# Reordering the opening, the first layers and the early bursts of a retention and two-layer kernel

## The chip, the cores and the metric

The kernel runs on one core of one Trainium2 chip. The metric is the device time of one execution in microseconds (us); less is better.

## The reference

```python
scores = (1/8) * q @ k.transpose(0, 1, 3, 2)          # 8 batches, 8 heads, 576 positions, 64 wide
gamma  = 1 - 2.0 ** (-5 - arange(8))                   # one decay per head
Dmat   = where(rel >= 0, gamma ** rel, 0)              # rel = i - j
x      = ((scores * Dmat) @ v) -> (4608 tokens, 512)
h      = x @ w_in                                      # 512 -> 2048
out    = maximum(0.01 * h, h) @ w_out                  # 2048 -> 512, float32
```

## The kernel before, in words

**Units and groups.** The 4608 tokens are cut into 36 units of 128 tokens (two chunks of 64) and into 9 groups of 4 units. A batch has nine chunks of 64, so a unit can straddle two batches; then each of its loads is two transfers. Retention is done chunk by chunk with a running state, all products are in float16 with float32 sums.

**Per unit u.** `load(u)` brings q, k and v in float32 (three transfers of 256 KB; `ld_pool` has six buffers). `cast_k` (L172, ScalarE) casts k, `cast_q` (L175) and `cast_v` (L179) multiply q and v by decay tables; q and k go to the tile `qk16`, v to `v16`. q and k are then transposed, in the opening by TensorE (`transpose_pe`, L200, with the copy `transposed`, L207), later by a DMA that SP issues (`transpose_dma`, L183). `scores(u)` (L215, L224) makes the 64-wide score blocks and the k-v products of both chunks in one PSUM tile. VectorE masks the scores (`masks`, L233) and advances the running state (`state`, L255, L257, L260, L261), and `state_cast` (L273, L276) makes it float16. The outputs need the mask, the state of the chunk before and the transposed q. Two forms exist: `outputs_acc` (L321, L333) sums both parts in PSUM and `x_copy` (L341, ScalarE) writes the tile `xT`; `outputs` (L291, L302) keeps the parts apart, ScalarE copies one (`own`, L355) and VectorE adds the other to it (`add`, L360), which gives `xT`.

**The two layers per group.** The first layer (L373) multiplies `w_in` with `xT` and ScalarE applies the leaky function (L387), giving `gt`. It comes in pieces: `h_block` (512 tokens), `h_half(g, a, fb)` (256 tokens: half a of group g; piece fb of the hidden width), `h_unit(u, fb)` (the 128 tokens of one unit, four column blocks, of group u // 4). The second layer of group 0 is the plain product `wide` (L423, 16 steps). Groups 1 to 8 use a seven-product scheme (`seven`, L483), with sums of weights (`mix_weights`, L448) and of activations (`mix`, L467) made by VectorE. After its first product ScalarE copies the sum out of PSUM (`keep("k1", "p1")`, L495), and the second product adds to the same PSUM tile, so it waits for that copy. Other results leave through L497, L506 and L508.

**What sets the order.** The schedule is written by hand: each engine runs its instructions in the order in which the code issues them, and waits where a value or a buffer is not ready. Buffers: `acc` (four PSUM tiles for transposes, fillers, first and second layer), `ot` and `sc` one PSUM tile each. `keep_warm(n)` issues n filler products on TensorE (L549, 128x512, no use of the result).

**Stages.** (1) The opening: units 0 to 3, with loads issued by SP and GpSimd, `w_in` in four quarters behind them on GpSimd's queue, and `w_out` last. (2) The first layers of groups 0 and 1, between which the units 4 to 7 are worked in: `turn(u, x)` transposes k (1) or q (0), `settle(u)` is state and mask, `finish(u)` is `outputs_acc` and `x_copy`. (3) `wide` and then `seven(1)`, with `ahead(u)` (casts by ScalarE and GpSimd, transpose by SP) and `burst(u)` (scores of u, outputs of u - 1, state, mask, own, add) placed between the products. Transfers of later units are issued by SP, in the order of the code: transposes, loads and stores share that queue. (4) Groups 2 to 8 in a loop, each with its four bursts. Units 8 to 11 are the tokens of group 2, so its first layer waits for the add of unit 11, which `burst(12)` holds.

The bursts of stage 3 stand as follows: unit 8 (scores only) after step 9 of `wide`; 9 after `wide`; 10, 11 and 12 after the products 1, 3 and 6 of `seven(1)` (counted from 0), the last being the final product. `ahead(u + 3)` and `load(u + 5)` follow each of the bursts 9 to 11.

Of the kernel before, what the change touches and what calls it, by code (L numbers as in the profile page):

```python
# [18 lines left out]
def kernel(  # L19
# [9 lines left out]
    nc = tc.nc  # L29
# [54 lines left out]
    def behind(dma, *others):  # L84
        for o in others:
            tc.add_manual_dep(
                dma.ins,
                o.ins.name,
                mybir.DependencyInfo(
                    mybir.DependencyClass.Sync, mybir.DependencyReason.DATA  # L90
                ),
                reason="order of loads",
            )
# [17 lines left out]
    last_load = {}  # L111
# [7 lines left out]
    def load(u, eng=None, after=None):  # L119
        for x in (1, 0, 2):  # L120
            t = ld_pool.tile([P, H, D], FP, name=f"t32_{x}")
            t32[u, x] = t
            c = 2 * u
            same = c % CB + 1 < CB
            e = eng[x] if isinstance(eng, dict) else eng or nc.sync
            engs = e if isinstance(e, tuple) else (e,)
            n = H // len(engs)
            for j, rows in ((0, P),) if same else ((0, CH), (1, CH)):
                b, w = (c + j) // CB, (c + j) % CB
                for i, e in enumerate(engs):  # L130
                    hs = slice(n * i, n * i + n)
                    d = e.dma_start(  # L132
                        out=t[CH * j : CH * j + rows, hs],
                        in_=(q, k, v)[x][b, hs, CH * w : CH * w + rows, :].rearrange(
                            "h t d -> t h d"
                        ),
                    )
                    if after is not None:
                        behind(d, *after)
                        after = None  # L140
                    last_load[u, x] = d

# [31 lines left out]
    def cast_q(u, eng):  # L174
        eng.tensor_tensor(out=qk16[u][:, 0], in0=t32[u, 0], in1=decay(u, 0), op=MUL)  # L175

    def cast_v(u, eng):
        v16[u] = a_pool.tile([P, H, D], F16, name="v16")
        eng.tensor_tensor(out=v16[u], in0=t32[u, 2], in1=decay(u, 1), op=MUL)  # L179
# [26 lines left out]
    def transposed(u, x, copy):  # L206
        copy(out=qkT[u][:, x], in_=tr[u, x])  # L207

    def scores(u):
        a = sc_pool.tile([P, 2, 2, NP, CH], FP, name="sc")  # L210
        sc_tiles[u] = a
        for p in range(NP):
            for g in range(2):
                for j in range(2):
                    nc.tensor.matmul(  # L215
                        out=a[half(j), g, 0, p, :],
                        lhsT=qkT[u][half(g), 1, p, half(j)],
                        rhs=qkT[u][half(g), 0, p, half(j)],
                        start=True, stop=True, skip_group_check=True,
                    )  # L220
        for p in range(NP):
            for j in range(2):
                for g in range(2):
                    nc.tensor.matmul(  # L224
                        out=a[half(g), j, 1, p, :],
                        lhsT=qk16[u][half(j), 1, 2 * p + g, :],
                        rhs=v16[u][half(j), 2 * p + g, :],
                        start=True, stop=True, skip_group_check=True,
                    )
# [316 lines left out]
    def keep_warm(n):  # L546
        t = acc_pool.tile([P, 1, TOK], FP, name="acc")
        for _ in range(n):
            nc.tensor.matmul(out=t[:, 0, :], lhsT=idle[:, 0:P], rhs=idle, start=True, stop=True)  # L549
# [7 lines left out]

    keep_warm(7)
    load(0, {1: nc.sync, 0: (nc.sync, nc.gpsimd), 2: nc.gpsimd})
    for u in range(1, 4):  # L560
        load(u, nc.gpsimd)
    for f in range(3):
        load_w_in(f)
    load(4, nc.gpsimd)
# [6 lines left out]
    cast_k(0)  # L571
    transpose_pe(0, 1)
    transposed(0, 1, act_copy)
    keep_warm(2)
    cast_q(0, nc.vector)
    cast_v(0, nc.vector)
    transpose_pe(0, 0)
    transposed(0, 0, act_copy)
    keep_warm(2)
    cast_k(1)  # L580
    cast_q(1, nc.vector)
    cast_v(1, nc.vector)
    for u in range(4):
        n = u + 1
        scores(u)
        state(u, 0)
        state_cast(u, dve_copy, (0,))
        masks(u)
        state(u, 1)
        if n < 4:  # L590
            transpose_pe(n, 1)
            transpose_pe(n, 0)
            transposed(n, 1, act_copy)
            transposed(n, 0, act_copy)
            keep_warm(1)
        if n < 3:
            cast_k(n + 1)
            cast_q(n + 1, nc.vector)
            cast_v(n + 1, nc.vector)
        state_cast(u, act_copy, (1,))  # L600
        if n < 4:
            outputs_acc(u)
            x_copy(u)
            keep_warm(2)
# [3 lines left out]
        for a, fb in items:  # L608
            h_half(g, a, fb)

    def casts(u, eng):
        cast_k(u)
        cast_q(u, nc.vector)
        cast_v(u, eng)

    def turn(u, x):
        transpose_pe(u, x)
# [2 lines left out]
    def settle(u):  # L620
        state(u, 0)
        state_cast(u, dve_copy, (0,))
        masks(u)
        state(u, 1)
        state_cast(u, act_copy, (1,))

    def finish(u):
        outputs_acc(u)
        x_copy(u)

    halves(0, (0, 0), (0, 1))
    finish(3)
    halves(0, (0, 2), (0, 3), (1, 0), (1, 1))
    casts(4, nc.vector)
    halves(0, (1, 2), (1, 3))
    turn(4, 1)
    halves(0, (0, 4), (0, 5))
    turn(4, 0)
    halves(0, (1, 4))
    casts(5, nc.vector)  # L640
    halves(0, (1, 5))
    scores(4)
    settle(4)
    halves(0, (0, 6), (0, 7))
    finish(4)
    turn(5, 1)
    halves(0, (1, 6))
    turn(5, 0)
    casts(6, nc.vector)
    halves(0, (1, 7))  # L650
    scores(5)
    settle(5)
    h_unit(4, 0)
    turn(6, 1)
    h_unit(4, 1)
    finish(5)
    turn(6, 0)
    casts(7, nc.vector)
    h_unit(5, 0)
    scores(6)  # L660
    settle(6)
    turn(7, 1)
    h_unit(5, 1)
    finish(6)
    halves(1, (0, 4))
    turn(7, 0)
    halves(1, (0, 5))
    scores(7)
    settle(7)
    halves(1, (0, 6))  # L670
    finish(7)
    load(8, after=(w_out_loads[2],))
    load(9)
    halves(1, (0, 7))
    for n in range(4):
        mix_weights(n, 0)
        mix_weights(n, 1)
        halves(1, (1, 2 * n), (1, 2 * n + 1))
# [34 lines left out]
    def step(u):  # L713
# [2 lines left out]
        ahead(u + 2)  # L716


    at = {
        0: lambda: (ahead(8), load(10)),  # L720
        3: lambda: (ahead(9), load(11)),
        6: lambda: (ahead(10), load(12)),
        9: lambda: (burst(8, False), ahead(11), load(13)),
        12: lambda: mixes(1, 0),
        14: lambda: mixes(1, 1),
    }
    for n in range(16):
        wide(n // 4, n % 4)
        if n in at:
            at[n]()  # L730

    def early(u):
        burst(u)
        if u < 12:
            ahead(u + 3)
            load(u + 5)

    early(9)
    mixes(1, 2)
    seven(  # L740
        1,
        {
            1: [lambda: early(10)],
            3: [lambda: early(11)],
            6: [lambda: early(12)],
        },
    )

    first = [f for i in range(4) for f in (i, i + HF)]
    second = [f for i in range(4, 8) for f in (i, i + HF)]  # L750
# [46 lines left out]
```

## Time and profile before

| | |
|---|---|
| median of 13 executions | 304.89 us (303.5 to 307.95) |
| the profiled execution | 304.37 us, of which the span of the trace is 302.6 |
| TensorE, matmuls | 286.0 us busy, 95% of the span |
| TensorE, weight loads | 193.5 us, 64% |
| VectorE | 169.9 us, 56% |
| ScalarE | 144.5 us, 48% |
| GpSimd | 106.0 us, 35% |
| mean granted TensorE clock | 0.977 of full |
| data moved | 50.01 MB, 165 GB/s |

The span runs from the first to the last instruction; the rest of the execution's time lies around it. PE is TensorE, PEld its weight load, DVE VectorE, ACT ScalarE, POOL GpSimd, SP the sync engine; a "q" behind an engine is its queue that issues transfers. L12 is line 12 of the kernel. In a timeline row the columns are start and length in us, engine, line, operation, result and operands, count, and in brackets the idle time of that engine before it with what ended it. Times in the text are from the start of the span.

### The profile page before, as it was taken

What the parts mean: (1) busy time and instruction counts of PE and PEld (TensorE: products, weight loads), DVE (VectorE), ACT (ScalarE), POOL (GpSimd) and SP (SyncE); (2) the same over time, 40 slices, a digit from 0 to 9 for tenths busy, and PEclk for the clock granted to TensorE, in tenths of its full rate; (3) what the DMA queues carried; (4) which work ended last, traced back from release to release, by engine and by line L of the source; (5) the groups of instructions that cost most, each with busy time, mean ns of one, the idle gap of its engine ahead of it and who ended that gap; (6) DMA issues with size and microseconds to landing.
All of it is one profiled execution on the core that took longest, in us unless ns stands there. A gap on an engine that the chain in (4) does not pass through costs nothing.

```text
span 302.6 us, 9351 instructions
## 1 busy us (share of the span) xinstructions
PE 286.0 (95%) x4068; PEld 193.5 (64%) x4068; DVE 169.9 (56%) x291; ACT 144.5 (48%) x254; POOL 106.0 (35%) x126
## 2 busy tenths in 40 slices
PE   7699987999996999999999999999999999999994
PEld 3358876854683458745864686478547854884583
DVE  2843475905994259545856564677458636740342
ACT  4646664643412773276237714762475167306510
POOL 8947901405643323433334333333334414000000
PEclk9859999999997999999999999999999999999999
DMA  7898999339999986896689767957896451012003
GB/s 205 240 197 176 312 207 221 69 79 237 247 239 209 310 182 142 183 254 140 135 193 250 163 149 213 217 131 167 220 220 109 97 175 37 4 42 99 0 2 139
DMA packets 130298, 50.01 MB, mean 165 GB/s; under 512 B 119728, under 2 KB 124464, under 8 KB 130256
## 3 DMA queue, kind: packets, MB, share of 16 engines
q1 hardware_dynamic: 123824, 39.20, 55.7%
q0 software_dynamic: 6144, 10.09, 15.1%
q8 instruction: 32, 0.52, 0.7%
q10 hardware_dynamic: 288, 0.11, 0.1%
q14 instruction: 10, 0.08, 0.1%
HBM read 36.81 MB, written 9.44 MB: 153 GB/s over the span
## 4 chain that ended last, share of the span: by engine, by line
PE 87%; DVE 3%; POOL 3%; DMA 2%; ACT 1%; issue 1%; DVEq 0%; ACTq 0%; POOLq 0%
PE acc L373 41%; PE acc L483 33%; PE acc L423 5%; POOL t L132 3%; PE sc L215 3%; DMA t<-in_v_dram 2%; PE sc L224 1%; PE ot L291 1%; PE ot L302 1%; DVE s L233 1%; PE ot L321 1%; DVE s L257 1%; ACT gt L387 0%; PE acc L200 0%; ACT k L495 0%
## 5 line engine op out<-in xcount | busy, mean ns | idle before, releaser
L373 PE MATMUL acc<-xT,w_in 128*128 128x512 f16 (+2 forms) x736 | 132.8, 337 | 3.7 <-DVE xT L360 2.8
L387 ACT ACTIVATE gt<-acc 128x512 f16<-128x512 f32 x144 | 85.6, 597 | 55.4 <-PE acc L373 54.0
L373 PEld LDWEIGHTS <-w_in 128*128 128x128 f16 x736 | 68.5, 99 | 57.1 <-issue 5.9
L483 PEld LDWEIGHTS <-gt 128*128 128x128 f16 x640 | 61.9, 98 | 10.8 <-issue 1.7
L233 DVE TENSOR_TENSOR s<-sc,cs 128x512 f16<-128x512 f32 x36 | 24.7, 685 | 47.5 <-PE sc L224 47.5
L483 PE MATMUL acc<-w_out,gt 128*128 128x256 f16 x384 | 45.9, 273 | 1.6 <-ACT k L495 1.4
L273 POOL CAST st<-s 128x512 f16<-128x512 f32 x21 | 12.8, 609 | 86.3 <-DVE s L257 55.9
L175 POOL TENSOR_TENSOR qk<-t,cs 128x512 f16<-128x512 f32 x28 | 30.1, 1074 | 30.4 <-DMA t<-in_q_dram 14.9
L355 ACT COPY own<-ot 128x512 f32<-128x512 f32 x28 | 16.4, 585 | 38.1 <-PE ot L302 30.5
L179 POOL TENSOR_TENSOR v<-t,cs 128x512 f16<-128x512 f32 x28 | 31.9, 1140 | 0.7 <-PE acc L373 0.4
L483 PE MATMUL acc<-w_mix,gt 128*128 128x256 f16 x256 | 30.6, 273 | 0.0
L467 DVE TENSOR_TENSOR mix<-gt 128x1024 f16<-128x1024 f16 x16 | 14.2, 891 | 28.8 <-ACT gt L387 28.8
L483 PE MATMUL acc<-w_mix,mix 128*128 128x256 f16 x256 | 29.3, 273 | 0.0
L172 ACT CAST qk<-t 128x512 f16<-128x512 f32 x36 | 22.3, 621 | 10.7 <-DMA t<-in_k_dram 10.7
L483 PEld LDWEIGHTS <-mix 128*128 128x128 f16 x256 | 25.0, 98 | 2.9
L360 DVE TENSOR_TENSOR xT<-ot,own 128x512 f16<-128x512 f32 x28 | 19.1, 682 | 0.3 <-ACT own L355 0.3
L257 DVE TENSOR_TENSOR s<-sc,s 128x256 f32<-128x256 f32 x40 | 16.7, 419 | 4.5 <-PE sc L224 4.0
L508 DVE TENSOR_TENSOR osb<-acc,u 128x512 f32<-128x512 f32 (+1 forms) x17 | 11.1, 656 | 9.0 <-PE acc L483 9.0
L215 PEld LDWEIGHTS <-qkT 64*64 64x64 f16 x576 | 7.8, 109 | 12.3 <-issue 10.1
L467 DVE TENSOR_TENSOR mix<-mix,gt 128x1024 f16<-128x1024 f16 x16 | 14.8, 932 | 0.5
L276 POOL CAST st<-s 128x256 f16<-128x256 f32 x7 | 3.2, 454 | 32.8 <-DVE s L261 18.2
L423 PE MATMUL acc<-w_out,gt 128*128 128x512 f16 x64 | 14.2, 379 | 0.0
(52 smaller groups left out, 245.6 us busy)
## 6 DMA issues: line engine op xcount, KB each, us to landing
out_dram<-osb SPq DMA_DIRECT2D x17, 512.0 KB, 3.8
t<-in_k_dram SPq DMA_DIRECT2D x26, 256.0 KB, 3.5
t<-in_q_dram SPq DMA_DIRECT2D x25, 256.0 KB, 4.0
t<-in_v_dram SPq DMA_DIRECT2D x25, 256.0 KB, 4.8
w_in<-in_moe_w_in_dram POOLq DMA_DIRECT2D x8, 256.0 KB, 9.1
w_out<-in_moe_w_out_dram POOLq DMA_DIRECT2D x4, 512.0 KB, 9.6
t<-in_v_dram POOLq DMA_DIRECT2D x7, 256.0 KB, 4.9
t<-in_k_dram POOLq DMA_DIRECT2D x6, 256.0 KB, 4.9
```

Of the source, the lines that this page charges most:

```text
L172: nc.scalar.copy(out=qk16[u][:, 1], in_=t32[u, 1])
L175: eng.tensor_tensor(out=qk16[u][:, 0], in0=t32[u, 0], in1=decay(u, 0), op=MUL)
L179: eng.tensor_tensor(out=v16[u], in0=t32[u, 2], in1=decay(u, 1), op=MUL)
L215: nc.tensor.matmul(out=a[half(j), g, 0, p, :], lhsT=qkT[u][half(g), 1, p, half(j)], rhs=qkT[u][half(g), 0, p, half(j)], start=True, stop=T ...
L233: nc.vector.tensor_tensor(out=s16s[u], in0=sc_tiles[u][:, :, 0], in1=mask_sb.unsqueeze(1).unsqueeze(1).to_broadcast([P, 2, NP, CH]), op=MUL,)
L257: nc.vector.tensor_tensor(out=to, in0=st, in1=carry[0], op=ADD)
L360: nc.vector.tensor_tensor(out=x_of(u).rearrange("q (c g) t -> q c g t", g=2), in0=ot_tiles[u][:, :, NP : 2 * NP].rearrange("q g (c j) t -> ...
L373: nc.tensor.matmul(out=hps[:, n, :], lhsT=w_in16[:, c, f * P : (f + 1) * P], rhs=xT[g][:, c, ts], start=(c == 0), stop=(c == NP - 1),)
L387: nc.scalar.activation(out=out, in_=in_, func=mybir.ActivationFunctionType.Lrelu)
L423: nc.tensor.matmul(out=ys[tb], lhsT=g_t[0][:, f, tb * P : (tb + 1) * P], rhs=w_out16[:, f, :], start=(f == 0), stop=(f == NF - 1),)
L467: nc.vector.tensor_tensor(out=z[:, fs], in0=a[:, fs], in1=b[:, fs], op=op)
L483: nc.tensor.matmul(out=r[name][:, tb, :], lhsT=lhs[:, f, tb * P : (tb + 1) * P], rhs=rhs[:, f, :], start=fresh and n == 0, stop=f == HF - ...
```

## The change

Loads of k for units 1 and 3 go from GpSimd's queue to SP's; that of unit 3 is issued when the one of unit 1 has landed. In the opening, VectorE casts q and v of unit 1 after state and mask of unit 0 and no longer before; TensorE does the outputs of unit 0 between the two transposes of unit 1; and there are 12 more fillers. Outputs of unit 3 stay where they were. For units 4 to 7, k is cast earlier, q and v casts follow the state and mask of the unit before, the float16 cast of the second chunk's state follows `x_copy`, and the places of some first-layer pieces change; two pieces `h_half(1, 1, 0)` and `(1, 1, 1)` become `h_unit(6, 0)` and `h_unit(7, 0)`. In stage 3, units 8 and 9 are prepared before `wide`, unit 8's burst stands after step 4 of `wide`, 9's after step 9, 10's after `wide`, and 11's and 12's after products 0 and 4 of `seven(1)`. Each `ahead` and `load` comes with its burst, so the cast of k of unit 13 now stands ahead of `seven(1)`. All other computation is the same.

```diff
@@ -135,8 +135,8 @@
                             "h t d -> t h d"
                         ),
                     )
-                    if after is not None:
-                        behind(d, *after)
+                    if after is not None and (x in after or not isinstance(after, dict)):
+                        behind(d, *(after[x] if isinstance(after, dict) else after))
                         after = None
                     last_load[u, x] = d
 
@@ -557,8 +557,9 @@
 
     keep_warm(7)
     load(0, {1: nc.sync, 0: (nc.sync, nc.gpsimd), 2: nc.gpsimd})
-    for u in range(1, 4):
-        load(u, nc.gpsimd)
+    load(1, {1: nc.sync, 0: nc.gpsimd, 2: nc.gpsimd})
+    load(2, nc.gpsimd)
+    load(3, {1: nc.sync, 0: nc.gpsimd, 2: nc.gpsimd}, {1: (last_load[1, 1],)})
     for f in range(3):
         load_w_in(f)
     load(4, nc.gpsimd)
@@ -571,34 +572,42 @@
     cast_k(0)
     transpose_pe(0, 1)
     transposed(0, 1, act_copy)
-    keep_warm(2)
+    keep_warm(3)
     cast_q(0, nc.vector)
     cast_v(0, nc.vector)
     transpose_pe(0, 0)
     transposed(0, 0, act_copy)
-    keep_warm(2)
+    keep_warm(3)
     cast_k(1)
-    cast_q(1, nc.vector)
-    cast_v(1, nc.vector)
     for u in range(4):
         n = u + 1
         scores(u)
+        if not u:
+            keep_warm(3)
         state(u, 0)
         state_cast(u, dve_copy, (0,))
         masks(u)
+        if not u:
+            cast_q(1, nc.vector)
+            cast_v(1, nc.vector)
         state(u, 1)
         if n < 4:
             transpose_pe(n, 1)
+            transposed(n, 1, act_copy)
+            if not u:
+                keep_warm(3)
+                outputs_acc(0)
+                x_copy(0)
+                keep_warm(1)
             transpose_pe(n, 0)
-            transposed(n, 1, act_copy)
             transposed(n, 0, act_copy)
-            keep_warm(1)
+            keep_warm(2 if not u else 3)
         if n < 3:
             cast_k(n + 1)
             cast_q(n + 1, nc.vector)
             cast_v(n + 1, nc.vector)
         state_cast(u, act_copy, (1,))
-        if n < 4:
+        if 0 < u < 3:
             outputs_acc(u)
             x_copy(u)
             keep_warm(2)
@@ -608,10 +617,9 @@
         for a, fb in items:
             h_half(g, a, fb)
 
-    def casts(u, eng):
-        cast_k(u)
+    def cast_qv(u):
         cast_q(u, nc.vector)
-        cast_v(u, eng)
+        cast_v(u, nc.vector)
 
     def turn(u, x):
         transpose_pe(u, x)
@@ -622,57 +630,64 @@
         state_cast(u, dve_copy, (0,))
         masks(u)
         state(u, 1)
-        state_cast(u, act_copy, (1,))
 
     def finish(u):
         outputs_acc(u)
         x_copy(u)
+        state_cast(u, act_copy, (1,))
 
     halves(0, (0, 0), (0, 1))
-    finish(3)
-    halves(0, (0, 2), (0, 3), (1, 0), (1, 1))
-    casts(4, nc.vector)
-    halves(0, (1, 2), (1, 3))
+    outputs_acc(3)
+    x_copy(3)
+    halves(0, (0, 2), (0, 3), (1, 0))
+    cast_k(4)
+    cast_qv(4)
+    halves(0, (1, 1), (1, 2), (1, 3))
     turn(4, 1)
     halves(0, (0, 4), (0, 5))
     turn(4, 0)
-    halves(0, (1, 4))
-    casts(5, nc.vector)
-    halves(0, (1, 5))
+    halves(0, (1, 4), (1, 5))
+    cast_k(5)
     scores(4)
     settle(4)
+    cast_qv(5)
     halves(0, (0, 6), (0, 7))
     finish(4)
     turn(5, 1)
+    cast_k(6)
     halves(0, (1, 6))
     turn(5, 0)
-    casts(6, nc.vector)
     halves(0, (1, 7))
     scores(5)
     settle(5)
+    cast_qv(6)
     h_unit(4, 0)
     turn(6, 1)
+    cast_k(7)
     h_unit(4, 1)
     finish(5)
     turn(6, 0)
-    casts(7, nc.vector)
     h_unit(5, 0)
     scores(6)
     settle(6)
+    cast_qv(7)
+    h_unit(5, 1)
     turn(7, 1)
-    h_unit(5, 1)
+    halves(1, (0, 4))
     finish(6)
-    halves(1, (0, 4))
     turn(7, 0)
     halves(1, (0, 5))
     scores(7)
     settle(7)
-    halves(1, (0, 6))
+    halves(1, (0, 6), (0, 7))
     finish(7)
     load(8, after=(w_out_loads[2],))
     load(9)
-    halves(1, (0, 7))
-    for n in range(4):
+    h_unit(6, 0)
+    mix_weights(0, 0)
+    mix_weights(0, 1)
+    h_unit(7, 0)
+    for n in range(1, 4):
         mix_weights(n, 0)
         mix_weights(n, 1)
         halves(1, (1, 2 * n), (1, 2 * n + 1))
@@ -716,35 +731,30 @@
         ahead(u + 2)
 
 
+    def early(u, out=True):
+        burst(u, out)
+        if 8 < u < 12:
+            ahead(u + 3)
+            load(u + 5)
+
+    ahead(8)
+    load(10)
+    ahead(9)
+    load(11)
     at = {
-        0: lambda: (ahead(8), load(10)),
-        3: lambda: (ahead(9), load(11)),
-        6: lambda: (ahead(10), load(12)),
-        9: lambda: (burst(8, False), ahead(11), load(13)),
-        12: lambda: mixes(1, 0),
-        14: lambda: mixes(1, 1),
+        2: lambda: (ahead(10), load(12)),
+        4: lambda: (burst(8, False), ahead(11), load(13)),
+        9: lambda: early(9),
+        11: lambda: mixes(1, 0),
+        13: lambda: mixes(1, 1),
     }
     for n in range(16):
         wide(n // 4, n % 4)
         if n in at:
             at[n]()
-
-    def early(u):
-        burst(u)
-        if u < 12:
-            ahead(u + 3)
-            load(u + 5)
-
-    early(9)
+    early(10)
     mixes(1, 2)
-    seven(
-        1,
-        {
-            1: [lambda: early(10)],
-            3: [lambda: early(11)],
-            6: [lambda: early(12)],
-        },
-    )
+    seven(1, {0: [lambda: early(11)], 4: [lambda: early(12)]})
 
     first = [f for i in range(4) for f in (i, i + HF)]
     second = [f for i in range(4, 8) for f in (i, i + HF)]
```

## The prediction

> **What bounds it.** I read the chain of waits first, then the wait before each TensorE group in the timeline, then the clock by microsecond. TensorE carries 87% of the chain, and from 25 us on it is nearly gapless, so only its gaps, its slow clock and the opening can give time. Columns of the chain: start, length, what.
>
> ```profile
> 1.27 8.80 POOL t L132 x10
> ...
> 10.07 6.96 DMA t<-in_v_dram
> ...
> 17.67 0.42 DVE s L257
> ```
>
> GpSimd issues ten loads, then unit 3's v lands at 17.03 and VectorE's state of unit 2 follows: the opening hangs on that load. The windows show (after the span and PE, PEld, DVE, ACT, POOL) the clock, DMA share and GB/s.
>
> ```profile
> 10.00:11.00 1.00, 0.00 (x0) 0.00 (x0) 0.97 (x3) 0.62 (x1) 1.00 (x2) 1.00 1.00 320
> ...
> 13.00:14.00 1.00, 1.00 (x9) 0.54 (x9) 0.92 (x3) 0.65 (x2) 1.00 (x2) 0.61 0.77 154
> ...
> 23.00:24.00 1.00, 1.00 (x8) 0.82 (x7) 0.97 (x3) 0.00 (x0) 0.67 (x1) 0.77 1.13 302
> ```
>
> ```profile
> 94.00:95.00 1.00, 0.00 (x0) 0.00 (x0) 0.97 (x3) 0.00 (x0) 0.62 (x1) 1.00 0.88 202
> ...
> 95.00:96.00 1.00, 0.45 (x2) 0.17 (x2) 0.50 (x1) 0.00 (x0) 0.61 (x1) 0.57 1.19 270
> ...
> 98.00:99.00 1.00, 1.00 (x5) 0.41 (x4) 0.00 (x0) 0.10 (x2) 0.00 (x0) 0.72 1.21 260
> ```
>
> TensorE idles at 10 us, the clock falls to half at 13.2 (0.61 of full in that slice) and is back at 23.46 (0.77); it falls again at 95.1 and is back at 98.56. The timeline gives the gaps (start, length; in brackets the idle time before and its releaser):
>
> ```profile
> 44.46 1.05 PE L373 MATMUL acc<-xT,w_in 128*128 128x128 f16 x16 [0.67 <-ACT xT L341]
> ...
> 48.30 0.31 PE L321 MATMUL ot<-s,v 64*64 64x64 f16 x8 [1.19 <-DVE s L233]
> ...
> 53.24 0.31 PE L321 MATMUL ot<-s,v 64*64 64x64 f16 x8 [0.55 <-DVE s L233]
> ```
>
> ```profile
> 78.03 0.62 ACT L172 CAST qk<-t 128x512 f16<-128x512 f32 x1
> ...
> 79.32 0.58 ACT L495 COPY k<-acc 128x512 f32<-128x512 f32 x1 [0.67 <-PE acc L483]
> ...
> 79.69 1.39 SPq L132 DMA_DIRECT2D t<-in_k_dram  x2
> ...
> 79.95 1.91 PE L483 MATMUL acc<-w_out,gt 128*128 128x256 f16 x16 [0.67 <-ACT k L495]
> ...
> 84.14 0.62 ACT L172 CAST qk<-t 128x512 f16<-128x512 f32 x1 [0.94 <-DMA t<-in_k_dram]
> ...
> 95.55 5.95 PE L373 MATMUL acc<-xT,w_in 128*128 128x512 f16 x20 [2.82 <-DVE xT L360]
> ```
>
> In the first layers 1.19 and 0.55 us go to late masks (units 6 and 7) and 0.67 to a late xT (unit 5). In the second stage product 1 waits 0.67 for ScalarE's copy of product 0, and the layer of group 2 starts 2.82 us late, behind the add of burst(12).
>
> **The skill.** "TensorE: Matmul & The Clock Gate", Part 1, says that a free-running window of about 3.4 us of low activity halves the clock. The trace agrees: 98.56 - 95.1 is one window, 23.46 - 13.2 = 10.2 is three. Its "Architectural detail" says that ScalarE and VectorE take instructions strictly in order; the lines above fit (the copy at 79.32 after the cast at 78.03), though that copy was waiting for TensorE, so this trace doesn't prove it. "DMA: Bandwidth & Descriptors", "Queues, rings and completion order", says that each engine takes one packet from each queue in turn. With both queues loaded, from 3.25 to 3.50 us:
>
> ```profile
> q10 hardware_dynamic: 91, 0.05, 65.6%
> ...
> q1 hardware_dynamic: 120, 0.03, 52.6%
> ```
>
> 91 packets against 120: near one for one, so it agrees.
>
> **Opening, part by part.** Moving k of units 1 and 3 to SP takes two issues (0.9 us each) off GpSimd, so v of unit 3 is issued at 8.3 instead of 10.07; with before's latencies (4.9 for q just ahead, 7.0 for it) it lands between 13.2 and 15.3. SP gains two issues, before the wait for load(8), which ends at 46.79: covered. k of unit 1 now shares the DMA engines with GpSimd's stream: behind 1,536 packets of unit 0 it starts at about 4.0; alone 1,024 packets need 1.0 us (272 per 0.25 us), in turn with GpSimd's 89 packets per us 11.5 us. GpSimd's stream shows a share of 0.956 where SP's shows 1.22, so there are free slots: I take 3.5 to 4 us, landing near 8, against 7.4 before. Its casts end near 8.7, TensorE wants it at 8.4.
>
> VectorE does unit 0's state and mask before unit 1's casts (timeline durations: state 0.42, its cast 0.29, mask 0.68, q and v casts 0.69): from scores at 7.7, mask(0) ends near 9.05 instead of 11.2. Then q1, v1, the state add, q2 and v2 end near 12.3; unit 1's state and mask to 14.55; q3 and v3 to 16.0 instead of 17.66. Outputs(2) can then start at 17.4, not 19.07. The 12 more fillers cost 0.21 each at full clock, 2.6 us, all in gaps where TensorE waits for masks or casts; behind them wait transposes and outputs, and without cover I would charge up to 0.6. They put five fillers in each stretch in which before had three or fewer, so the clock should hold. In the half-clock stretch from 19.07 to 23.46 that is worth about 2.0.
>
> What is late next is w_in. GpSimd's issues wait for its landings:
>
> ```profile
> 19.56 0.68 POOL L132 DMA_DIRECT2D t<-in_q_dram  x1 [1.55 <-DMA w_in<-in_moe_w_in_dram]
> ...
> 20.77 0.68 POOL L132 DMA_DIRECT2D t<-in_q_dram  x1 [0.52 <-DMA w_in<-in_moe_w_in_dram]
> ...
> 23.34 0.69 POOL L132 DMA_DIRECT2D t<-in_v_dram  x1 [0.63 <-DMA w_in<-in_moe_w_in_dram]
> ```
>
> Quarter 0 is there at 20.77, quarter 1 at 23.34. It is issued 1.85 us earlier; shared engines give it, I estimate, 0 to 1 us. Then h_half(0,2) begins at 22.4 to 23.4 instead of 25.42: gain 2.0 to 3.0, taken **2.5**. Later loads follow w_in by up to 1 us; k, q, v of unit 5 land at 32.7 to 34.3 and are wanted at 33.7 at the earliest, still covered.
>
> **Units 4 to 7.** q and v casts move behind the state and mask, k casts ahead, state casts behind x_copy. In the coordinates of before: xT(5) is copied at 43.45 instead of 43.82, h_unit(5,0) starts at 44.05 (0.4 gained). Scores(6) are followed by 2.16 us of products instead of 1.3, so outputs(6) start at 47.9, not 48.3. The moved casts come back as waits: q7 is cast at 48.9, so turn(7,0) is 0.15 late, and scores(7) at 50.5 wait 0.4 for the copy behind v7. Outputs(7) then start at 52.6 with one 0.87 us half more done. Two h_units replace two halves (1.07 against 0.87 each, +0.4) but hide the xT(7) wait. The six halves end at 60.85 instead of 62.33: **-1.45**.
>
> **Wide product and sevens.** The bursts come earlier, so own(11) and add(11) run under two products (3.5 us): the 2.82 us go. But SP's issues hardly move. From transpose 8 at 63.71 SP is busy without a break to 84; only the store of 0.85 us moves behind load 13. So load 13 is issued at 78.6, its second half at 79.3, and lands 3.6 us later: 82.9. ScalarE casts it (0.62), and only then copies p1 for "k1" (0.58), because ahead(13) now stands before the sevens: 84.3. The second product needs that copy; TensorE is ready after product 0 and burst(11) at about 81.1. So **a new wait of some 3.2 us** takes the place of the old one, plus 0.8 at burst(9), whose outputs(8) need GpSimd's state cast behind v10 (70.93 + 1.04, then 0.6). From 84.35: six products of 1.77 and burst(12), 0.64, end at 95.6, against 95.55. **+0.05**, before the clock. Bursts 13 on keep their place.
>
> Clock: before lost half of 95.55 to 98.56, 1.5 us. The new gap, 80.5 to 84.35 with one burst in it, drops the clock for a window (1.7) in about half of its phases[...]: 0.85. **-0.65**. Bounds of this stage: -4.3 if k13 comes in time, +1.7 if it lands 1 us later and the clock falls.
>
> **Sum.** -2.5 - 1.45 + 0.05 - 0.65 = -4.55. The profiled execution took 304.37 (span 302.6, 1.77 around it), so 299.8; the median of the runs, 304.89, stands 0.5 above it: **300.3**. A measurement of this kernel can tell about 0.5% (1.5 us) from no change.
>
> **Rivals.** (1) k of unit 1 starves on SP's queue, one packet per GpSimd packet: it lands near 15.5, unit 1's scores go to 19, outputs(2) to 24.2, h_half(0,2) to 28.5 (+3.1), with one more half-clock window (1.7): 304.9 + 3.1 + 1.7 - 1.45 - 0.65 = 307.6, slower. The packet counts above speak for it, the free slots against. It decides from a landing at about 13 on. (2) k of unit 13 is cast in time: waits of 3.5 and 1.5 of clock go, with opening and units 4 to 7: 304.9 - 2.5 - 1.45 - 3.5 - 1.5 = 296.0. Against it: 0.94 us waited for that landing already before. (3) The clock still falls in the opening, or w_in comes no sooner and the v3 gain is eaten: 0.8 instead of 2.5, 302.0. For it: the seven fillers that before has from 4.8 to 12.6 us did not hold the clock. Against it: twice as many stand there now. That the change doesn't do what it says: the earlier transposes lie behind the same SP queue; that is inside the main case.
>
> **Chances.** Main 0.46 (its own range 298.5 to 302), (2) 0.13, (3) 0.25, (1) 0.16. Of (3), a third lies within 0.5%. Faster: 0.46 + 0.13 + 0.16 = 0.75; same 0.09; slower 0.16. The range 296.0 to 304.5 leaves out (1) and little else.
>
> **What would show it.** Right: clock 1.0 from 13 to 23 us, first w_in product before 21 us, masks(6) and (7) without a wait on TensorE, the wait before group 2 gone, and a wait of about 3 us on ScalarE's p1 copy, itself behind a cast that waits for DMA of k. Wrong: ScalarE's cast of unit 1 waiting past 10 us, a half clock before 23 us, or no wait at the second product.

## The result and the profile after

The kernel after takes **300.49 us** in the median (296.11 to 303.5, 11 executions), where the kernel before, run beside it, takes 305.04 (302.11 to 307.95, 48 executions). The ratio is **0.982**, with a 95% interval from 0.978 to 0.986: faster, by 4.6 us of medians. This ratio, like every one below, is taken over the faster executions, those within 1.5% of the fastest of their kernel, and so lies below the 0.985 that the two medians give. The profiled execution of after took 301.37 us (span 299.6), so it is 0.9 above its own median, while before's was 0.7 below: the two traces differ by only 3.0 us. Spans are compared with spans below, and medians with medians.

Split at the same places, the two traces give this (us):

| stretch | before | after | difference | the prediction's sum |
|---|---|---|---|---|
| start to `h_half(0, 2)` | 25.43 | 21.90 | -3.53 | -2.5 |
| to the first step of `wide` | 36.90 | 36.23 | -0.67 | -1.45 |
| to the first product of group 2 | 33.22 | 36.04 | +2.82 | +0.05, and +0.85 for the clock |
| from there to the end | 207.05 | 205.43 | -1.62 | -1.5 |
| sum | 302.6 | 299.6 | -3.0 | -4.55 |

**The opening.** In the chain of waits of after (start, length, what), the issues and the late v of unit 3, which led before, are gone. The first q leads, and VectorE's masks and casts follow from 5.7 to 14 us:

```profile
1.27 4.39 DMA t<-in_q_dram
...
9.36 0.59 DVE s L233
```

The cast of unit 3's v stands at 15.26 instead of 17.06, without a wait, outputs(2) at 17.35 instead of 19.07 and the first product with `w_in` (L373) at 19.16 instead of 21.96. GpSimd's issues that wait for `w_in` show the same two landings as in the prediction's fence: quarter 0 is there at 17.19 instead of 20.77, quarter 1 at 19.59 instead of 23.34. From the timeline of after, the cast, the issue that waits for quarter 1, and `h_half(0, 2)`:

```profile
15.26 0.68 DVE L179 TENSOR_TENSOR v<-t,cs 128x512 f16<-128x512 f32 x1
...
19.59 0.72 POOL L132 DMA_DIRECT2D t<-in_v_dram  x1 [0.58 <-DMA w_in<-in_moe_w_in_dram]
...
21.90 4.28 PE L373 MATMUL acc<-xT,w_in 128*128 128x256 f16 x35
```

The windows of after (last three columns: clock, DMA share, GB/s) have the full clock in the slices where before had 0.61 and 0.77; TensorE, idle at 10 us before, is busy for 0.91 of that slice now:

```profile
13.00:14.00 1.00, 0.85 (x7) 0.34 (x5) 0.96 (x4) 0.98 (x3) 0.70 (x1) 1.00 1.12 156
...
23.00:24.00 1.00, 1.00 (x11) 0.88 (x9) 0.00 (x0) 0.97 (x3) 1.00 (x2) 1.00 1.15 222
```

**The first layers.** The timeline of TensorE shows the waits for the masks of units 6 and 7 gone (the second is the line at 50.20 below, which has no bracket) and that for xT of unit 5 down to 0.35. But three gaps come up that nothing in the trace explains: a short one ahead of 24.27 us (0.12 us between products), and the two here that are marked "issue":

```profile
40.43 0.22 PE L321 MATMUL ot<-s,v 64*64 64x64 f16 x3 [0.38 <-issue]
...
47.10 0.94 PE L373 MATMUL acc<-xT,w_in 128*128 128x256 f16 x7 [0.78 <-issue]
...
50.20 0.31 PE L321 MATMUL ot<-s,v 64*64 64x64 f16 x8
```

**Wide product and sevens.** The wait of 2.82 us ahead of group 2 is gone: the product at 94.17 stands without a bracket. Others have come. From the timeline of after, all engines:

```profile
75.66 2.39 SPq L132 DMA_DIRECT2D t<-in_k_dram  x2
...
79.22 0.32 PE L215 MATMUL sc<-qkT 64*64 64x64 f16 x16 [2.28 <-DMA qkT<-qk]
80.49 0.62 ACT L172 CAST qk<-t 128x512 f16<-128x512 f32 x1 [3.71 <-DMA t<-in_k_dram]
...
81.02 0.58 ACT L495 COPY k<-acc 128x512 f32<-128x512 f32 x1
...
81.65 3.20 PE L483 MATMUL acc<-w_out,gt 128*128 128x256 f16 x16 [1.63 <-ACT k L495]
```

Read it from the bottom: the second product waits 1.63 us for the copy at 81.02, which stands behind the cast of unit 13's k at 80.49, which waited 3.71 us for its load, issued at 75.66. Ahead of it, scores(11) wait 2.28 us for unit 11's transpose, issued at 73.72 and there 5.5 us later. With 0.51 us at scores(10) and 0.25 at outputs(9) the waits are 4.67 us together, against 3.49 in before (0.67 and 2.82). They lie close together, with little work between, and the clock falls:

```profile
80.00:81.00 1.00, 0.02 (x1) 0.04 (x1) 1.00 (x3) 0.51 (x1) 0.00 (x0) 0.96 0.92 209
81.00:82.00 1.00, 0.35 (x2) 0.26 (x2) 0.97 (x3) 1.00 (x3) 0.00 (x0) 0.50 0.72 163
...
84.00:85.00 1.00, 1.00 (x9) 0.83 (x8) 0.00 (x0) 0.00 (x0) 1.00 (x2) 0.83 1.24 237
```

Half speed from 80.92 to 84.33 is 3.41 us, one window as "TensorE: Matmul & The Clock Gate" (Part 1) in the Trainium skill has it. TensorE waits until 81.65 anyway, so the half clock costs it half of the 2.68 us of work that follow, 1.34. With the 1.18 of waits that makes 2.52 of the stage's +2.82. The other 0.30 stand in no bracket: product 0 begins at 75.02 and takes 1.77 us, so scores(11) come 2.43 us late and not 2.28. An estimate from this: 0.15 us more at each wait, and four waits where before has two, gives the 0.30.

Over whole executions the window shows as a step: the mean granted clock takes a few values, some 0.0055 apart (half of a window of 3.41 us, in 300 us), and the time goes with it, though not in equal steps. Where the window lies is known for the profiled execution alone. Eleven executions of after and its profiled one: 296.1 us at clock 1.0 (one), 299.7 at 0.994 (mean of five), 301.0 at 0.989 (five), 303.5 at 0.983 (one). Medians below are mixtures of such steps.

### The profile page after: what moved, and what is told of

It is laid out like the page before. It is cut to its first block, busy times and chain, and to the rows that moved or that the text cites. A ratio compares the mean times of both kernels' runs of the same rounds, so it can differ in the third digit from the quotient of the medians.

```text
span 299.6 us, 9407 instructions
## 1 busy us (share of the span) xinstructions
PE 285.2 (95%) x4096; PEld 193.3 (65%) x4096; DVE 168.4 (56%) x291; ACT 143.9 (48%) x254; POOL 103.4 (35%) x124
## 4 chain that ended last, share of the span: by engine, by line
PE 85%; DMA 5%; SPq 3%; DVE 2%; issue 2%; ACT 1%; POOL 0%; DVEq 0%; POOLq 0%; ACTq 0%
PE acc L373 42%; PE acc L483 33%; PE sc L215 3%; DMA t<-in_q_dram 2%; DMA t<-in_v_dram 2%; SPq L132 2%; SPq L183 1%; PE ot L321 1%; PE sc L224 1%; PE ot L291 1%; PE ot L302 1%; PE acc L200 1%; PE acc L549 1%; PE ot L333 1%; DVE qk L175 0%
## 5 line engine op out<-in xcount | busy, mean ns | idle before, releaser
L373 PE MATMUL acc<-xT,w_in 128*128 128x512 f16 (+2 forms) x752 | 130.8, 329 | 1.2 <-issue 0.8
L373 PEld LDWEIGHTS <-w_in 128*128 128x128 f16 x752 | 68.0, 98 | 53.2 <-issue 1.8
L483 PE MATMUL acc<-w_out,gt 128*128 128x256 f16 x384 | 47.2, 277 | 2.5 <-ACT k L495 2.3
L175 POOL TENSOR_TENSOR qk<-t,cs 128x512 f16<-128x512 f32 x28 | 29.5, 1053 | 35.8 <-DMA t<-in_q_dram 35.8
L273 POOL CAST st<-s 128x512 f16<-128x512 f32 x21 | 13.3, 631 | 82.2 <-DVE s L257 53.7
L215 PE MATMUL sc<-qkT 64*64 64x64 f16 x576 | 11.5, 198 | 3.1 <-DMA qkT<-qk 2.8
```

Source lines behind the costliest of these rows:

```text
L215: nc.tensor.matmul(out=a[half(j), g, 0, p, :], lhsT=qkT[u][half(g), 1, p, half(j)], rhs=qkT[u][half(g), 0, p, half(j)], start=True, stop=T ...
L373: nc.tensor.matmul(out=hps[:, n, :], lhsT=w_in16[:, c, f * P : (f + 1) * P], rhs=xT[g][:, c, ts], start=(c == 0), stop=(c == NP - 1),)
L483: nc.tensor.matmul(out=r[name][:, tb, :], lhsT=lhs[:, f, tb * P : (tb + 1) * P], rhs=rhs[:, f, :], start=fresh and n == 0, stop=f == HF - ...
```

## The experiments

Each kernel's ratio is to the kernel before on the same chip, with a 95% interval. "Stage 3" is the stretch from the first step of `wide` to the first product of group 2.

### The parts alone

The first three kernels each take one part of the change and leave the rest as before.

The opening alone, edit against before:

```diff
-    for u in range(1, 4):
-        load(u, nc.gpsimd)
+    load(1, {1: nc.sync, 0: nc.gpsimd, 2: nc.gpsimd})
+    load(2, nc.gpsimd)
+    load(3, {1: nc.sync, 0: nc.gpsimd, 2: nc.gpsimd}, {1: (last_load[1, 1],)})
...
-        if n < 4:
+        if 0 < u < 3:
             outputs_acc(u)
```

> Only the opening (loads, units 0 to 3, fillers) as changed, the rest as before. My theory: the opening gives its part by itself, h_half(0,2) at about 22 us instead of 25.4, so 3.0 to 3.5 us off before (301.5). If the parts only work together (the gain is swallowed by a later wait for w_in, w_out or unit 5's loads), less than 1 us. If the gain is the clock alone, the start of the layers moves by 2 us and half-clock windows go from the opening, but the state of unit 2 is no earlier than 17.6.

Measured: 300.93 us, ratio 0.989 (0.983 to 0.994), about -3.5 us. `h_half(0, 2)` begins at 22.00, as in after. The wait ahead of group 2 is there as in before, but in this trace the clock stayed full through it:

```profile
93.17 4.48 PE L373 MATMUL acc<-xT,w_in 128*128 128x512 f16 x20 [2.79 <-DVE xT L360]
```

The layers alone, edit against before:

```diff
-    halves(0, (0, 2), (0, 3), (1, 0), (1, 1))
-    casts(4, nc.vector)
-    halves(0, (1, 2), (1, 3))
+    halves(0, (0, 2), (0, 3), (1, 0))
+    cast_k(4)
+    cast_qv(4)
+    halves(0, (1, 1), (1, 2), (1, 3))
...
```

> Only the layers of units 4 to 7 as changed. My theory: the six last halves end 0.7 to 1.5 us earlier, 304.0 in the median. Rival: the moved q and v casts cost what the later state casts give, no change (305).

Measured: 302.09 us, ratio 0.991 (0.988 to 0.994), about -2.7 us. From `h_half(0, 2)` at 25.19 to `wide` at 59.69 it takes 34.50 us, 2.4 less than before: no wait of TensorE there is left but one gap of 0.20. So the layers are worth more than the 0.67 that the trace of after shows; that trace lost it to its gaps.

Stage 3 alone, edit against before:

```diff
     at = {
-        0: lambda: (ahead(8), load(10)),
...
+        4: lambda: (burst(8, False), ahead(11), load(13)),
+        9: lambda: early(9),
...
-            1: [lambda: early(10)],
-            3: [lambda: early(11)],
-            6: [lambda: early(12)],
+    seven(1, {0: [lambda: early(11)], 4: [lambda: early(12)]})
```

> Only wide product, seven products and bursts as changed. My theory: the wait of 2.8 us before group 2 goes and waits for qkT(11) and for the copy of product 0 behind the cast of k13 come, 3 to 4.5 us together, so between 0.5 us faster and 2 us slower than before (304.5 to 307). Rival, that the bursts ahead are what made the change faster: 3 to 4 us faster, 301 to 302.

Measured: 305.96 us, ratio 1.000 (0.996 to 1.003); the medians alone put it 1.2 us above before. Stage 3 takes 36.28 us, 3.06 more than before. The waits are of the same kinds as in after, 4.22 us together, but spread otherwise: scores(11) wait 1.01 us, and 1.36 go to GpSimd's state casts. The second product waits for the copy (85.02), which stands behind the cast of k13 (84.49), which waited 3.15 us for its load. Its timeline:

```profile
85.64 3.56 PE L483 MATMUL acc<-w_out,gt 128*128 128x256 f16 x16 [1.85 <-ACT k L495]
```

The three ratios multiply to 0.979, and the whole is 0.982 (0.978 to 0.986). The opening and the layers are the whole gain; the part that took the largest wait away is worth nothing that can be measured.

### What carries the opening

k of units 1 and 3 back on GpSimd's queue, the rest as after:

```diff
-    load(1, {1: nc.sync, 0: nc.gpsimd, 2: nc.gpsimd})
-    load(2, nc.gpsimd)
-    load(3, {1: nc.sync, 0: nc.gpsimd, 2: nc.gpsimd}, {1: (last_load[1, 1],)})
+    for u in range(1, 4):
+        load(u, nc.gpsimd)
```

> The changed kernel with k of units 1 and 3 back on GpSimd's queue. My theory: v of unit 3 lands near 17 again, unit 2's state starts at 17.7 instead of 15.9 and the layers start 1.5 to 2 us later: 302. Rival: the order on VectorE and the fillers gave all of the opening's gain: 300.5 as with the loads on SP.

Measured: 302.2 us, ratio 0.988 (0.985 to 0.992), against 0.982 (0.978 to 0.986) for after: the intervals overlap. In the trace the edit is worth 0.72 us: `h_half(0, 2)` begins at 22.62 instead of 21.90, not the 1.5 to 2 us later that I expected. Its timeline:

```profile
21.82 0.68 POOL L132 DMA_DIRECT2D t<-in_v_dram  x1 [0.58 <-DMA w_in<-in_moe_w_in_dram]
```

The cast of v3 stands at 16.06, only 0.8 later. Quarter 1 of `w_in` has moved by 2.23 (21.82 against 19.59), more than the two issues of 0.9 that now stand ahead of it, and is still 0.8 us ahead of its use. So `w_in` does not bind, with or without these issues. The kernel's median stands 1.7 above that of after; the remaining 1 us is not traced to this edit, and its profile also has two half-clock windows in stage 3 instead of one. That the median came out at my 302 is in good part luck.

After with the filler counts of before:

```diff
-    keep_warm(3)
+    keep_warm(2)
...
-        if not u:
-            keep_warm(3)
...
-                keep_warm(1)
...
-            keep_warm(2 if not u else 3)
+            keep_warm(2 if not u else 1)
```

> The changed kernel with the opening's fillers in the numbers of before (2, 2, 1, 2 and so on, 12 fewer). My theory: in most executions the clock falls in the opening for one to three windows, 1 to 2.5 us slower than the changed kernel (302). Rival: the new order alone leaves no long gap, the clock holds and the time is the same or 0.3 less.

Measured: 302.15 us, ratio 0.994 (0.991 to 0.997), a little above the 0.990 that the medians give. After has 0.982 and 0.985: by the ratios the intervals are apart, by the medians of all executions the distance is 1.7 us. The clock is lost from 8 to 15 us, by its windows:

```profile
14.00:15.00 1.00, 0.68 (x9) 0.29 (x9) 1.00 (x3) 1.00 (x3) 0.64 (x2) 0.50 1.23 204
15.00:16.00 1.00, 0.92 (x33) 0.66 (x31) 0.96 (x3) 0.69 (x3) 0.59 (x2) 1.00 1.28 215
```

With the new order and the moved loads it is back at 15 instead of 23.46, and `h_half(0, 2)` begins at 22.82. So in the trace the twelve fillers are worth 0.92 us and the move of k 0.72. The other 1.9 of the 3.5 us are left to the new order of VectorE's and TensorE's work. That is a subtraction, which takes it that the three simply add; the order has no run of its own.

### Where the gain of stage 3 went

The first test: `ahead(13)` and `load(15)` move behind product 0's copy, so that ScalarE copies first and casts k13 then.

```diff
-    early(10)
+    burst(10)
     mixes(1, 2)
-    seven(1, {0: [lambda: early(11)], 4: [lambda: early(12)]})
+    seven(
+        1,
+        {
+            0: [lambda: (ahead(13), load(15)), lambda: early(11)],
+            4: [lambda: early(12)],
+        },
+    )
```

> The changed kernel with ahead(13) and load(15) behind product 0's copy, so that ScalarE no longer casts k13 ahead of it. My theory: the 1.6 us of the second product's wait go, those for qkT(10) and qkT(11) (0.8 and 2.3) stay; 1 to 2 us faster than the changed kernel, 299, and fewer half-clock windows. Rival (the copy isn't what binds, transposes are): the same time as the changed kernel, 300.5, with the wait moved to another transpose.

Measured: 298.54 us, ratio 0.980 (0.973 to 0.986), 2 us of median under after, though the intervals overlap. The trace shows it plainly. Stage 3 is 34.43 us, 1.61 shorter; the copy is at 75.14 and nothing waits for it. The wait ahead of it stays (timeline of TensorE and ScalarE):

```profile
75.14 0.58 ACT L495 COPY k<-acc 128x512 f32<-128x512 f32 x1
...
77.18 0.32 PE L215 MATMUL sc<-qkT 64*64 64x64 f16 x16 [2.08 <-DMA qkT<-qk]
```

So the 1.63 us were the cast ahead of the copy. What is left is the late transpose, 0.62 us for GpSimd's state cast behind it, and a half-clock window from 78.8 to 82.2.

The next two tried to cure the loads: loads 10 to 13 directly behind load 9, so that SP issues them long before the transposes; the second of them adds the copy-first edit just shown.

```diff
     load(9)
+    for u in range(10, 14):
+        load(u)
...
-        4: lambda: (burst(8, False), ahead(11), load(13)),
+        4: lambda: (burst(8, False), ahead(11)),
```

> The changed kernel with the loads of units 10 to 13 issued directly behind those of unit 9, where SP lay idle from 50.5 to 59.5 us, and no longer between the transposes. My theory: transposes 10 to 13 no longer stand behind loads on SP, k13 is there long before its cast; the waits of 0.8, 2.3 and 1.6 us and a half-clock window go: 4 to 6 us faster than the changed kernel, 295. Rival: the transposes themselves (5 to 6 us to landing) bind whatever SP does: 1 us or less. Second rival: the early loads delay w_out and units 8 and 9, no gain.

> As the kernel with early loads, and ahead(13) behind product 0's copy too. My theory: with k13 loaded early its cast costs ScalarE only 0.6 us ahead of the copy, and that under burst(11); so no difference to the kernel with early loads (295), within 0.5. Rival: the copy is still late there: 0.5 to 1 us faster.

Measured: 305.0 and 304.57 us, ratios 1.001 (0.998 to 1.004) and 1.000 (0.998 to 1.003): all that the other parts give is lost. My theory that early loads help fell; that the copy makes no difference beside them, 0.43 us of median, held. The timeline of the first shows why (SP's queue, then TensorE):

```profile
48.30 2.32 SPq L132 DMA_DIRECT2D t<-in_k_dram  x1
...
68.94 4.12 SPq L183 DMA_TRANSPOSE qkT<-qk  x3
...
72.37 0.43 PE L215 MATMUL sc<-qkT 64*64 64x64 f16 x16 [10.60 <-DMA qkT<-qk]
```

SP needs from 46 to 68.9 us for six loads: with the transfers under way, single issues stretch from 0.4 to 2.3 us. The next three transposes stand behind all of them, and scores(8) wait 10.60 us. Early loads are not free on a queue that the transposes share.

### The old bursts, and one product between

With after's opening and layers, stage 3 of before is put back:

```diff
     at = {
+        0: lambda: (ahead(8), load(10)),
...
-    seven(1, {0: [lambda: early(11)], 4: [lambda: early(12)]})
...
+            1: [lambda: early(10)],
+            3: [lambda: early(11)],
+            6: [lambda: early(12)],
```

> The opening and the layers of the kernel after, with the kernel before's bursts and loads in the wide stage and the seven products. Theory (the bursts brought ahead cost about 2.8 us by putting new waits ahead of the transposes, and the other two parts are the whole gain): the stage from the first wide product to the first product of group 2 takes 33 to 33.5 us instead of 36.04, with one wait of about 2.8 us ahead of group 2 and no wait at the second product; the clock falls once near that wait; median 297.3 to 298.5 us, about 2 to 3 below the kernel after. Rival (the bursts ahead are needed, since the earlier start leaves less time for the loads, so the wait ahead of group 2 grows): the stage takes 35 to 36 us and the median is 300 to 301.

Measured: 300.12 us, ratio 0.982 (0.977 to 0.986): the same as after. Half of the theory held: stage 3 takes 33.10 us, with the old wait ahead of group 2, 2.67 us from 87.7 on, and the 0.67 at the second product. The wait in the timeline, and a slice of it in the windows (TensorE at nothing, clock at 1.00):

```profile
90.35 4.48 PE L373 MATMUL acc<-xT,w_in 128*128 128x512 f16 x20 [2.67 <-DVE xT L360]
...
89.00:90.00 1.00, 0.00 (x0) 0.00 (x0) 0.97 (x3) 0.00 (x0) 0.85 (x2) 1.00 1.08 227
```

The other half failed: the time is not 2 to 3 us below after. The six executions suggest why. The profiled one, with the full clock all through that wait, took 297.64. The other five had a clock of 0.992 to 0.994 and took 299.38 to 300.98, 2.5 us more in the mean. If their lost clock lies behind this wait, which their means don't show, then the clock falls after most waits of this length and costs about as much as the wait. The last kernel below tests it.

Two kernels, run beside it, put one product between. The first takes the last burst one product earlier, so that product 6 lies between the work of VectorE in that burst and the layer that needs it:

```diff
             3: [lambda: early(11)],
-            6: [lambda: early(12)],
+            5: [lambda: early(12)],
```

> e9_old_bursts with the burst of unit 12 one product earlier (behind product 5 instead of 6), so that product 6 lies between its activations and the first product of group 2. Theory (the 2.8 us ahead of group 2 is VectorE's chain behind burst 12, and one product of 1.77 us covers as much of it): the wait shrinks to about 1.0 us, the clock no longer falls there, median 1.5 to 2.5 us below e9_old_bursts, about 295.5 to 296.5, below both kernels. Rival (the q and k transposes of unit 12 or its state come late, so the wait moves to scores(12)): the same as e9_old_bursts within 0.5 us, with 1.5 to 2 us of wait at scores(12).

Measured: **296.7 us**, ratio **0.972** (0.968 to 0.976), below both kernels: after's interval begins at 0.978, that of the old bursts at 0.977. The wait splits into two, one of them the transpose of unit 12 (timeline of TensorE):

```profile
85.91 0.32 PE L215 MATMUL sc<-qkT 64*64 64x64 f16 x16 [1.04 <-DMA qkT<-qk]
...
89.44 4.48 PE L373 MATMUL acc<-xT,w_in 128*128 128x512 f16 x20 [0.96 <-DVE xT L360]
```

In sum they are 2.00 us instead of 2.67, and stage 3 is 32.64 us, only 0.46 shorter. Yet the median is 3.4 lower, more than the 1.5 to 2.5 that I expected. All six executions have a clock of 0.999 or 1.0 (296.39 to 297.75), and the two profiled executions, both at full clock, are only 1.0 apart (297.64 and 296.63): most of the gain is the window that doesn't fall, not the wait. The rival had a part in it too: half of the wait did move to scores(12).

The second takes the copy-first kernel and puts burst 11 behind product 1:

```diff
-            0: [lambda: (ahead(13), load(15)), lambda: early(11)],
+            0: [lambda: (ahead(13), load(15))],
+            1: [lambda: early(11)],
             4: [lambda: early(12)],
```

> e4_copy_first with the burst of unit 11 behind product 1 instead of product 0. Theory (scores(11) waits about 2.1 us because its transpose lands late by the time, not by what is ahead of it on TensorE): product 1 of 1.77 us lies over it, the wait falls to 0.3 to 0.6 us, about 0.3 to 0.6 us of wait for ScalarE's copy comes back at the second product, median 297.0 to 297.7. Rival (the loads behind burst 11 go out later too and the next wait grows by as much, at scores(12) or ahead of group 2): 298.3 to 299.0, no change from e4_copy_first.

Measured: 297.66 us, ratio 0.975 (0.971 to 0.979), as the theory had it in time: 0.9 below copy first, though on another chip and with overlapping intervals. The waits are now three, none long:

```profile
74.89 1.91 PE L483 MATMUL acc<-w_out,gt 128*128 128x256 f16 x16 [0.69 <-ACT k L495]
...
78.81 0.26 PE L302 MATMUL ot<-qkT,st 64*64 64x64 f16 x8 [1.25 <-POOL st L273]
...
85.46 0.32 PE L215 MATMUL sc<-qkT 64*64 64x64 f16 x16 [1.05 <-DMA qkT<-qk]
```

The wait of scores(11) is gone, but outputs(10) and scores(12) now wait over 1 us each, as the rival had it in part. Together that is 2.99 us, where the old bursts have 3.34, of which 2.67 lie in one piece. Stage 3 is 33.13 us, the same as the 33.10 there; and the clock is 0.997 to 1.0 in all six, and the median 2.5 lower.

The last kernel takes the clock by itself: the old bursts with ten fillers in the wait, which end nothing earlier.

```diff
+    keep_warm(10)
     first = [f for i in range(4) for f in (i, i + HF)]
```

> e9_old_bursts with ten fillers (0.21 us each, 2.1 in all) on TensorE in the 2.7 us in which it waits for add(11) ahead of group 2; the wait's end doesn't move, since VectorE sets it. Theory (in 5 of 6 runs of e9_old_bursts this wait also cost a half-clock stretch, of some 2.4 us: 297.6 at full clock against 300.0 for the others): the clock holds, most runs lie at 297.4 to 298.2, median 2 to 2.5 us below e9_old_bursts, though nothing ends earlier in the stage (33.1 us, the wait that is left 0.3 to 0.7). Rival (the runs of e9_old_bursts differ for another reason, in the transfers): median 299.7 to 300.4 as e9_old_bursts, though the wait is filled; up to 0.4 more if the fillers outlast the wait.

Measured: 298.45 us (297.17 to 299.44), ratio 0.978 (0.973 to 0.983), against 300.12 and 0.982 (0.977 to 0.986) without fillers: 1.7 lower in the median, a little less than I expected, on another chip and with overlapping intervals. The clock is 0.997 to 1.0 in all six executions, where it was 1.0 in one of six. TensorE still starts group 2 when VectorE is done, and stage 3 is 33.29 us:

```profile
88.55 2.33 PE L549 MATMUL acc<-idle 128*128 128x512 f16 x10
91.50 4.48 PE L373 MATMUL acc<-xT,w_in 128*128 128x512 f16 x20 [0.62 <-DVE xT L360]
```

That the fillers hold the clock is shown; what it is worth is 1.7 us here and 2.5 between the executions of the old bursts. One window can cost at most 1.7, half of its length. What makes up the rest of the 2.5 stays open.

What the last three kernels share can be read from the windows of all the traces: how long TensorE is busy within any 3.41 us of stage 3. At the emptiest place it is 2.37 us with burst 12 earlier, 2.04 with burst 11 behind product 1 and 2.74 with the fillers, and none of their 18 executions has a mean clock under 0.997; the little that is missing lies, in their traces, at the very end of the span, where TensorE has nothing to do. The kernel before has a place with 0.59, after 0.79, the opening alone 0.62 and the old bursts 0.74; the clock fell there in the first two traces and held in the other two. The opening fits too: in before the 3.41 us ahead of the fall at 13.22 have 1.90, without the twelve fillers those ahead of 8.17 have 1.80, and the emptiest place in the opening of after has 2.77.

## Why the prediction was right, and where it was not

The forecast of 300.3 us met 300.49. The causes that it named were right; the sizes of its terms were off in both directions, and that they met in the median is luck.

- **Opening: right in mechanism, too small.** The late v of unit 3, the late masks and the half clock went as said, and k of unit 1 came in time (its cast at 7.35 us without a wait), so rival 1 fell. The packet counts that spoke for that rival were of SP's queue and ScalarE's, in one quarter of a microsecond; from 4 to 7 us in after SP's queue moved 1,066 packets and GpSimd's 196, not one for one. Rival 3 fell as well, with the clock at 1.00 and `w_in` sooner. The term that was mis-sized is "What is late next is w_in": quarters 0 and 1 came 3.6 and 3.75 us sooner, not "0 to 1 us", and `w_in` never bound. Hence 3.53 instead of 2.5. Without this cap the prediction's own path is close: outputs(2) came 1.72 us earlier (1.67 in its sum), and from there to `h_half(0, 2)` it takes 1.81 less (about 2.0). The step took account of the 1.85 us of earlier issue and not of the stream that the quarters stand in; putting the two issues back moved them by 2.1 to 2.2. The other 1.5 have no run of their own.
- **Fillers: right that the clock holds.** Twelve more hold it, and without them it is half from 8 to 15 us. The 2.0 us that I put on the half clock were too many for them alone: 0.92, since the rest of the new opening ends the half clock 8 us sooner by itself.
- **Units 4 to 7: right within the scatter.** I said -1.45 (the two times in the prediction give 1.48). Ten traces of kernels with after's layers and its opening, or nearly, take 34.8 to 36.2 us for this stretch (after 36.23, copy first 35.19, the old bursts 35.35), 35.4 in the mean, against 36.90, 36.94 and 37.15 in the three traces with the old layers; the layers alone take 34.50. That is -0.7 to -2.4 against before, and -1.5 in the mean of the ten. The waits left as I said (masks of 6 and 7 none, xT(5) 0.35 of 0.67); what scatters are the gaps marked "issue". Their cause is not in the trace and wasn't tried.
- **Stage 3: the new wait was right, and not all of it.** The cast of k13 ahead of the copy was named, and taking it away gave 1.6 us of the stage. But I had 3.2 us for it. The step that failed is "TensorE is ready after product 0 and burst(11)": it lets burst(11) run straight behind product 0, and scores(11) wait there 2.28 us for their own transpose; behind that the copy's wait is only 1.63. The waits came to 4.67, against 4.0 in my sum (3.2 and 0.8), and the stage without the half clock to +1.48 (2.82 less 1.34) instead of "+0.05". The lower bound "-4.3" is not what rival 2 takes off for the same case, 3.5 and 1.5.
- **Clock in stage 3: the half chance was too low.** I put 0.85 us on the new gap for "about half of its phases". It fell in the trace and cost 1.34, and 11 of the 12 executions of after have a clock under 1.0. Most of the 1.5 won behind the start of group 2 (1.62 measured) is paid back in front of it: stage 3 and clock together gave 1.20 us more instead of 0.6 less, against the 1.0 that the opening gave beyond its term.
- **The sum.** -3.0 in the traces against -4.55: +1.8 from stage 3 and the clock, +0.8 from units 4 to 7, -1.0 from the opening. That the medians still differ by 4.6 is chance: the profiled execution of after lies 0.9 above its median and that of before 0.7 below, which makes up the same 1.55.
- **Rival 2** (k13 in time, 296.0) is not refuted for each execution: the one at full clock took 296.11. It has no trace, so whether k13 came in time there stays open.

Open too: why the DMA engines nearly rest from 70.5 to 72.75 us in after (18 GB/s in the mean, against 242 from 69 to 70 and 283 from 73 to 74), and whether a second queue for the transposes would end the waits of stage 3. Neither was tried.

## What to carry to other kernels

Where a matrix engine's clock falls in windows, the price of a wait is its length plus half of the time that the engine then works at half clock (here 1.34 us, at most 1.7). So look for the emptiest stretch of the window's length, here 3.41 us, and spread a wait that can't be removed over two or three places with a product between, before trying to shorten it. An engine that copies a result for the next product should do so ahead of any cast that waits for a load: the copy here takes 0.58 us and held TensorE up for 1.63 through the order alone. And before bringing loads forward, read the issuing queue: what shares it, transposes above all, moves back by as much.

## What the runs showed of the hardware

- Whether a wait drops the clock depends on more than its length: 2.82 us did (before), 2.50 (the layers alone), 2.67 and 2.79 did not in their traces, and the kernel with the 2.67 us wait, judged by the mean clock, lost a window in five of six executions. Three waits of 0.69 to 1.25 us, 2.99 in all, did not.
- What the traces have in common: in the 3.41 us ahead of each of the twelve falls of the clock before the last products, over all traces, TensorE was busy for 1.90 us or less (0 to 1.90). One long wait is not needed for that: the longest ahead of the fall at 13.22 us in before is 1.73 us. And a place with less need not make the clock fall: the old bursts have one with 0.74.
- The issue of a 256 KB load on SP took 0.37 to 2.32 us, the longest while the transfers ahead were still under way; six loads held SP's queue for 23 us.
- A load of small packets (256 bytes) on SP's queue did not starve beside GpSimd's stream: k of unit 1, issued at 1.86 us in after, was there by 7.35, and SP's queue moved five packets for each one of GpSimd's meanwhile (1,066 and 196 from 4 to 7 us).
